# Seven block products instead of eight in a gated-MLP kernel's spatial product, with the gate branch moved ahead of it and staged in DRAM

## Chip, cores and metric

One core of one Trainium2 chip. The metric is the device time of one execution in microseconds (us). The span that a profile gives is 1.8 us shorter than the time of its run. Most runs of a kernel agree within 1%.

## The reference

```python
x = A_x                                  # (1, 2048, 576) bf16
xn = layernorm(x)
s = irfft2(rfft2(xn) * (w_r + 1j * w_i)) # a spectral filter, in six steps p0 to p5 of the kernel
z = gelu(xn @ w_in)                      # w_in: 576 x 4608
z1, z2 = z[..., :2304], layernorm(z[..., 2304:])
g = w_sp @ z2 + b_sp[:, None]            # w_sp: 2048 x 2048, the spatial product
out = x + s * silu((z1 * g) @ w_out)     # w_out: 2304 x 576
```

The spatial product is 2048 x 2048 x 2304, by far the largest of the four.

## The kernel before

z2 is computed first and stays in SBUF. The spatial product runs for four quarters of the output positions (512 columns each) and 18 feature blocks of 128. Each of these 72 steps also computes its own block of z1 one step ahead; the filter's last steps p4 and p5 fill the first steps.

```python
def z1(k):                                   # 5 matmuls of 512 columns
    ...
    nc.scalar.activation(out=Z1T[k % 3], in_=ph[:], func=ACT.Gelu_apprx_tanh)

def main(k, between=()):                     # 16 matmuls of 512 columns
    q, fi = steps[k]
    pg = psh.tile([P, 512], F32, tag="h")
    for m in range(MT):
        ...
        nc.tensor.matmul(pg[:], lhsT=Z2[m][:, fi * P:(fi + 1) * P], rhs=SLAB[q % 2][:, m, :],
                         start=(m == 0), stop=(m == MT - 1))
    nc.vector.tensor_tensor(out=tmp, in0=pg[:], in1=BB[:, q * 512:(q + 1) * 512], op=ALU.add)
    nc.vector.tensor_tensor(out=U[k % NU], in0=tmp, in1=Z1T[k % 3], op=ALU.mult)
# ... schedule, cut:
for k in range(NK):                          # 72 steps
    units = au[3 * k:3 * k + 3]              # p4 and p5 of the filter, in the first 10 steps
    ...
    if q + 1 < NQ and fi >= sl0 and fi < sl0 + 4:
        load_slab(q + 1, [fi - sl0])         # transposing loads of w_sp, into the other of two buffers
    if k + 1 < NK:
        z1(k + 1)
    main(k, units[1:])
    if fi == 0 and q > 0:
        for i in range(4):
            outm(q - 1, i)                   # 36 matmuls of 288 columns, then tanh, s and x
```

Of the kernel before, what the change touches and what calls it, by code (L numbers as in the profile page):

```python
# [79 lines left out]
def kernel(  # L80
# [25 lines left out]
    NQ = S // 512  # L106
# [18 lines left out]
    Yd = dram.tile([S, D], BF16)  # L125

# [5 lines left out]
    xnT = pers.tile([P, MT, KS, P], BF16)  # L132
    Z2 = [pers.tile([P, Fh], BF16, name=f"z2_{m}") for m in range(MT)]
    RW = pers.tile([P, KS * Fh], BF16)
# [10 lines left out]
    sizes = dict(A0=12288, G4=N2 * P, CESO=NLC * 2 * L, MM=3 * P, XN=3 * KS * P, STG=6 * L,  # L145
                 AIN=4 * 8 * L, PAD=3568, TT=8 * L, BES=2 * 8 * L, ZT=4 * 512)
# [6 lines left out]
    def reg(name, off, n):  # L153
# [7 lines left out]
    SLAB = [reg("AIN", 2 * 8 * L, 8192).rearrange("p (m t) -> p m t", m=MT),  # L161
            reg("A0", 0, 8192).rearrange("p (m t) -> p m t", m=MT)]
# [8 lines left out]
    BB = reg("TT", 0, S)  # L171
    BES = [reg("BES", i * 8 * L, 8 * L) for i in range(2)]
    WIN1 = [reg("BES", i * KS * WG * P, KS * WG * P).rearrange("p (k f) -> p k f", k=KS) for i in range(2)]
    Z1T = [reg("ZT", i * 512, 512) for i in range(3)]
    TMP = [reg("ZT", 3 * 512, 512), reg("BES", 2 * KS * WG * P, 512)]
    WOUT = reg("A0", 8192, FT * D).rearrange("p (f d) -> p f d", f=FT)
    fin = [reg("A0", 8192 + FT * D + i * D, D) for i in range(6)]
    YIN, XIN, GO = fin[0:2], fin[2:4], fin[4:6]
    WIN2 = RW[:].rearrange("p (k f) -> p k f", k=KS)
    NU = KS * Fh // 512  # L180
    U = [RW[:, i * 512:(i + 1) * 512] for i in range(NU)]

    warm = Z2[MT - 1][:, 0:512]
# [127 lines left out]
    def p4_read(ch):  # L311
        nc.sync.dma_start(out=AIN[ch % 2], in_=rowv(Ed)[:, ch * 8 * L:(ch + 1) * 8 * L])

    def p4(u):
        ch, lc = u // NLC, u % NLC
        av = AIN[ch % 2].rearrange("p (s l) -> p s l", s=8)
        pa = psa.tile([P, 2, 4, P], F32, tag="a")
        for i in range(8):
            nc.tensor.matmul(pa[:, i // 4, i % 4, :], lhsT=av[:, i, LC0[lc]:LC0[lc] + P], rhs=G4[:, ch * 8 + i, :],  # L319
                             start=True, stop=True)  # L320
        vd = V[:, lc, :, ch * 8:ch * 8 + 8, :].rearrange("p c s t -> p s c t")
        vs = pa[:].rearrange("p a s (c t) -> p (a s) c t", c=2)
        if u % 2 == 0:
            nc.vector.tensor_copy(out=vd, in_=vs)
        else:
            nc.scalar.activation(out=vd, in_=vs, func=ACT.Identity)
        if lc == NLC - 1 and ch < 2:
            p4_read(ch + 2)
# [3 lines left out]
    def p5(j):  # L332
        pa = psa.tile([P, 2, 512], F32, tag="a")
        for c in range(2):
            for lc in range(NLC):
                nc.tensor.matmul(pa[:, c, 0:L], lhsT=V[:, lc, c, 2 * j:2 * j + 2, :], rhs=CESO[:, lc, c, :],  # L336
                                 start=(lc == 0), stop=(lc == NLC - 1))
        ob = TH[:, j % 2, 0:L]
        nc.scalar.activation(out=ob, in_=pa[:, 1, 0:L], func=ACT.Identity)
        y = STG[j % 3][:, 0:D]  # L340
        nc.vector.tensor_tensor(out=y[:, 0:L], in0=pa[:, 0, 0:L], in1=ob, op=ALU.add)
        nc.vector.tensor_tensor(out=y[:, L:D], in0=pa[:, 0, H2 - 1:0:-1], in1=TH[:, j % 2, H2 - 1:0:-1], op=ALU.subtract)
        for h in range(2):
            nc.sync.dma_start(out=Yv[2 * j + h], in_=y[h * N1:(h + 1) * N1, :])

    junk = TH[:].rearrange("p a d -> p (a d)").bitcast(BF16)
# [4 lines left out]
    def z2(u):  # L351
# [10 lines left out]
        zc = Z2[m][:, n * ZC:(n + 1) * ZC]  # L362
        if on_act:
            nc.scalar.activation(out=zc, in_=ph[:], func=ACT.Gelu_apprx_tanh, accum_out=st[:, n:n + 1])  # L364
            if n % 2 == 1:
                i = NZC + n // 2
                nc.scalar.activation(out=junk[:, 0:2 * ZC], in_=Z2[m][:, (n - 1) * ZC:(n + 1) * ZC], func=ACT.Square,  # L367
                                     accum_out=st[:, i:i + 1])
        else:
            nc.scalar.activation(out=zc, in_=ph[:], func=ACT.Gelu_apprx_tanh)  # L370
            stats_q.append((u, partial(nc.vector.bn_stats, out=st[:, n, :], in_=zc)))
# [3 lines left out]
    stats_q = []  # L375

    def z2_norm(m, st, on_act):
# [9 lines left out]
        else:  # L387
            nc.vector.bn_aggr(out=mv[:, 0, :], in_=st[:])
        rs = rstd_of(mv, 1, "l2")
        stats_q.append((m * NZC + NZC + 1, partial(nc.vector.tensor_scalar, out=Z2[m][:], in0=Z2[m][:], scalar1=mv[:, 0, 0:1],  # L390
                                                   scalar2=rs[:], op0=ALU.subtract, op1=ALU.mult)))

# [6 lines left out]
    def load_slab(q, parts=range(4)):  # L399
        for i in parts:  # L400
            t0 = q * 512 + i * P
            nc.sync.dma_start_transpose(out=SLAB[q % 2][:, :, i * P:(i + 1) * P], in_=wspv[t0:t0 + P, :, :])

    steps = [(q, fi) for q in range(NQ) for fi in range(FT)]

    def z1(k):
        q, fi = steps[k]
        g = (q * FT + fi) // WG
        wb = WIN1[g % 2]
        ph = psh.tile([P, 512], F32, tag="h")  # L410
        for ks in range(KS):
            nc.tensor.matmul(ph[:].rearrange("p (a t) -> p a t", a=4), lhsT=wb[:, ks, (fi % WG) * P:(fi % WG + 1) * P],  # L412
                             rhs=xnT[:, 4 * q:4 * q + 4, ks, :], start=(ks == 0), stop=(ks == KS - 1))
        nc.scalar.activation(out=Z1T[k % 3], in_=ph[:], func=ACT.Gelu_apprx_tanh)  # L414

    def main(k, between=()):
        q, fi = steps[k]
        between = list(between)
        pg = psh.tile([P, 512], F32, tag="h")
        for m in range(MT):  # L420
            if m % 8 == 0 and between:
                between.pop(0)()
            nc.tensor.matmul(pg[:], lhsT=Z2[m][:, fi * P:(fi + 1) * P], rhs=SLAB[q % 2][:, m, :],  # L423
                             start=(m == 0), stop=(m == MT - 1))
        tmp = TMP[k % 2]
        nc.vector.tensor_tensor(out=tmp, in0=pg[:], in1=BB[:, q * 512:(q + 1) * 512], op=ALU.add)  # L426
        nc.vector.tensor_tensor(out=U[k % NU], in0=tmp, in1=Z1T[k % 3], op=ALU.mult)  # L427

    def load_xy(m):
        nc.sync.dma_start(out=YIN[m % 2], in_=Yd[m * P:(m + 1) * P, :])  # L430
        nc.sync.dma_start(out=XIN[m % 2], in_=xv[:, m, :])

    def outm(q, i):
        m = 4 * q + i
        b = m % 2
        cols = [(0, D)] if m < MT - 1 else [(0, H2), (H2, H2 + H2 // 2), (H2 + H2 // 2, D)]
        for c0, c1 in cols:
# [4 lines left out]
            for fi in range(FT):  # L442
                for h in range(nh):
                    nc.tensor.matmul(pv[:, h, :], lhsT=U[(q * FT + fi) % NU][:, i * P:(i + 1) * P],  # L444
                                     rhs=WOUT[:, fi, c0 + h * H2:c0 + h * H2 + w // nh], start=(fi == 0), stop=(fi == FT - 1))
# [5 lines left out]
            nc.sync.dma_start(out=out2[m * P:(m + 1) * P, c0:c1], in_=GO[b][:, c0:c1])  # L451
        if i < 2:
            load_xy(m + 2)
# [7 lines left out]
    NK = len(steps)  # L461
    zq = iter(range(MT * NZC))

    def fill(n, norm=True):
        for u in zq:
            z2(u)
            if norm:
                z2_stats(u)
            n -= 1
            if n == 0:  # L470
                break
# [27 lines left out]
    with tc.manual_schedule(engines={SP, PE, DVE}):  # L499
# [3 lines left out]
        load_w(1)  # L503
        fill(14)
# [9 lines left out]
        for hh in range(0, N2, 2):  # L514
# [3 lines left out]
            fill(1)  # L518
            p3(hh)
            if hh % 4 == 2 and hh >= 16:  # L520
                load_slab(0, [hh // 4 - 4])
        for i in range(2):
            nc.gpsimd.memset(WIN1[i][KT:P, KS - 1, :], 0.0)
        p4_read(0)
        p4_read(1)
        load_win1(0)
        load_win1(1)
        nc.sync.dma_start(out=BB, in_=B_b_sp.rearrange("(a s) -> a s", a=1).to_broadcast((P, S)))
        fill(MT * NZC)
        z2_stats(MT * NZC)  # L530
        z1(0)
        au = [partial(p4, u) for u in range(4 * NLC)] + [partial(p5, j) for j in range(MT)]
        LAST = (len(au) - 1) // 3
        for k in range(NK):
            q, fi = steps[k]
            units = au[3 * k:3 * k + 3]
            if units:
                units[0]()
            if k == LAST + 1:
                nc.sync.dma_start(out=WOUT, in_=B_w_out.rearrange("(f p) d -> p f d", p=P))  # L540
            sl0 = LAST + 2 if q == 0 else 2
            if q + 1 < NQ and fi >= sl0 and fi < sl0 + 4:
                load_slab(q + 1, [fi - sl0])
            if k + 1 < NK:
                z1(k + 1)
            z2_stats(MT * NZC + 9 * (k + 1))
            main(k, units[1:])
            if fi % WG == 1 and k // WG + 2 < NK // WG:
                load_win1(k // WG + 2)
            if fi == FT - 2:  # L550
                load_xy(4 * q)
                load_xy(4 * q + 1)
            if fi == 0 and q > 0:
                for i in range(4):
                    outm(q - 1, i)
        for i in range(4):
            outm(NQ - 1, i)


# [28 lines left out]
```

## Time and profile before

| | before |
|---|---|
| time, median of the first 4 runs | 552.93 us |
| span of the profiled run, granted clock | 551.1 us, 0.998 |
| TensorE busy | 540.0 us (98%), 3156 matmuls |
| VectorE busy | 221.6 us (40%) |
| spatial product | 1152 matmuls at 215.9 ns, 248.7 us |

Busy time of TensorE overstates the work, because the ends of pipelined matmuls are modelled. What counts is the distance from one matmul's start to the next (its pitch).

### The profile page before, as it was taken

The numbers are of one execution on the slowest core, as the hardware profiler recorded it, in microseconds if no ns is written. First come the engines' busy times: TensorE is split into PE (matmuls) and PEld (weight loads), VectorE is DVE, ScalarE is ACT, GpSimd is POOL, SyncE is SP. The second block draws the span as 40 slices with busy tenths as digits, with TensorE's granted clock in tenths as the row PEclk, the third lists the DMA queues.
The fourth block names the chain that finished last, engine by engine and source line by source line (L and its number), as shares of the span: only waits on it lengthen the run. The fifth ranks groups of instructions, "written<-read, shape, count | busy, mean of one in ns | idle before, by whom it ended". The sixth has DMA issues, their size and how long they took to land.

```text
span 551.1 us, 7917 instructions
## 1 busy us (share of the span) xinstructions
PE 540.0 (98%) x3156; PEld 300.2 (54%) x3156; DVE 221.6 (40%) x440; ACT 169.8 (31%) x353; POOL 41.5 (8%) x105
## 2 busy tenths in 40 slices
PE   6999999999999999999999999999999999999997
PEld 3876656665555544476444446744444574444465
DVE  5914678968545522223222222322222233222224
ACT  4788887875332211111111110111111111111101
POOL 3852111111000000000000000000000000000000
PEclk9999999999999999999999999999999999999999
DMA  9826489996304397213811120283111121112002
GB/s 307 274 88 233 166 230 267 204 205 193 119 23 101 99 272 154 75 34 91 180 33 32 33 75 2 87 179 71 32 33 44 32 76 43 33 33 77 0 1 86
DMA packets 77813, 59.50 MB, mean 108 GB/s; under 512 B 37200, under 2 KB 71888, under 8 KB 77520
## 3 DMA queue, kind: packets, MB, share of 16 engines
q1 hardware_dynamic: 76864, 56.60, 37.9%
q0 software_dynamic: 768, 2.37, 1.4%
q8 instruction: 24, 0.39, 0.3%
q14 instruction: 13, 0.11, 0.1%
q10 hardware_dynamic: 144, 0.03, 0.0%
HBM read 38.78 MB, written 11.82 MB: 92 GB/s over the span
## 4 chain that ended last, share of the span: by engine, by line
PE 88%; ACT 4%; DVE 2%; DMA 2%; issue 1%; POOL 1%; SPq 0%; DVEq 0%; POOLq 0%
PE pg L423 45%; PE ph L412 14%; PE po L444 12%; PE ph L360 8%; PE pa L251 3%; PE pa L336 2%; ACT z L364 2%; DMA AR<-in_A_w_i_dram 1%; ACT TH L367 1%; PE pa L319 1%; DMA AR<-in_A_x_dram 1%; PE pl L444 1%; PE pb L305 1%; PE pt L242 1%; ACT AR L271 1%
## 5 line engine op out<-in xcount | busy, mean ns | idle before, releaser
L423 PE MATMUL pg<-AR,z 128*128 128x512 bf16 x1152 | 261.7, 379 | 0.0
L423 PEld LDWEIGHTS <-z 128*128 128x128 bf16 x1152 | 112.3, 98 | 132.3
L426 DVE TENSOR_TENSOR AR<-pg,AR 128x512 bf16<-128x512 f32 x72 | 49.8, 692 | 212.3 <-PE pg L423 212.3
L414 ACT ACTIVATE AR<-ph 128x512 bf16<-128x512 f32 x72 | 43.0, 597 | 236.9 <-PE ph L412 236.7
L412 PE MATMUL ph<-xnT,AR 128*128 128x512 bf16 x360 | 89.5, 379 | 0.0
L360 PE MATMUL ph<-RW,xnT 128*128 128x384 bf16 x480 | 87.0, 326 | 0.0
L444 PE MATMUL po<-AR,RW 128*128 128x288 bf16 x540 | 66.8, 286 | 0.0
L444 PEld LDWEIGHTS <-RW 128*128 128x128 bf16 x594 | 56.9, 98 | 14.6
L360 PEld LDWEIGHTS <-xnT 128*128 128x128 bf16 x480 | 46.9, 98 | 26.9
L412 PEld LDWEIGHTS <-AR 128*128 128x128 bf16 x360 | 35.0, 98 | 39.8
L427 DVE TENSOR_TENSOR RW<-AR 128x512 bf16<-128x512 bf16 x72 | 30.6, 426 | 6.6
L447 ACT ACTIVATE TH<-po 128x576 f32<-128x576 f32 x15 | 9.8, 652 | 73.9 <-PE po L444 73.9
L370 ACT ACTIVATE z<-ph 128x384 bf16<-128x384 f32 x54 | 25.8, 489 | 12.3 <-PE ph L360 12.3
L448 DVE SCALAR_TENSOR_TENSOR AR<-TH,po 128x576 bf16<-128x576 f32 x15 | 11.3, 754 | 44.9 <-ACT TH L447 44.9
L395 DVE BATCH_NORM_STATS2 st<-z 128x6 f32<-128x384 bf16 x54 | 26.9, 545 | 0.9 <-ACT z L370 0.7
L295 DVE TENSOR_TENSOR AR<-pa,AR 128x578 bf16<-128x578 f32 x32 | 22.7, 748 | 5.1 <-DMA AR<-in_A_w_r_dram 2.3
L251 PE MATMUL pa<-AR,xnT 128*128 128x289 bf16 x160 | 22.7, 288 | 1.6 <-ACT xnT L243 1.6
L364 ACT ACTIVATE z<-ph 128x384 bf16<-128x384 f32 x42 | 20.3, 485 | 5.7 <-PE ph L360 5.3
L395 DVE TENSOR_SCALAR z<-z,mv,rs 128x2304 bf16<-128x2304 bf16 x16 | 14.0, 876 | 10.6 <-POOL rs L213 10.6
L251 PEld LDWEIGHTS <-xnT 128*128 128x128 bf16 x160 | 15.0, 98 | 5.7 <-ACT xnT L243 2.0
L367 ACT ACTIVATE TH<-z 128x768 bf16<-128x768 bf16 x21 | 17.7, 843 | 0.6
L213 POOL TENSOR_TENSOR rs<-ve,mhalf 128x1 f32<-128x1 f32 x30 | 16.7, 556 | 2.4
(57 smaller groups left out, 262.2 us busy)
## 6 DMA issues: line engine op xcount, KB each, us to landing
AR<-in_B_w_in_dram SPq DMA_DIRECT2D x24, 384.0 KB, 3.6
AR<-in_A_x_dram SPq DMA_DIRECT2D x20, 144.0 KB, 3.3
AR<-in_B_w_out_dram SPq DMA_DIRECT2D x1, 2592.0 KB, 9.6
Ad<-AR POOLq DMA_DIRECT2D x16, 144.5 KB, 3.5
AR<-Ad SPq DMA_DIRECT2D x4, 578.0 KB, 5.8
AR<-in_A_w_r_dram SPq DMA_DIRECT2D x16, 144.5 KB, 5.0
AR<-in_A_w_i_dram SPq DMA_DIRECT2D x16, 144.5 KB, 3.9
Bd<-AR SPq DMA_DIRECT2D x4, 578.0 KB, 2.8
```

The costliest lines, as they stand in the source:

```text
L251: nc.tensor.matmul(pa[:, c, 0:L], lhsT=xnT[:, m, ks, :], rhs=CDSD[:, ks, c, :], start=(ks == 0), stop=(ks == KS - 1))
L360: nc.tensor.matmul(ph[:], lhsT=xnT[:, m, ks, :], rhs=WIN2[:, ks, n * ZC:(n + 1) * ZC], start=(ks == 0), stop=(ks == KS - 1))
L364: nc.scalar.activation(out=zc, in_=ph[:], func=ACT.Gelu_apprx_tanh, accum_out=st[:, n:n + 1])
L367: nc.scalar.activation(out=junk[:, 0:2 * ZC], in_=Z2[m][:, (n - 1) * ZC:(n + 1) * ZC], func=ACT.Square, accum_out=st[:, i:i + 1])
L370: nc.scalar.activation(out=zc, in_=ph[:], func=ACT.Gelu_apprx_tanh)
L395: stats_q.pop(0)[1]()
L412: nc.tensor.matmul(ph[:].rearrange("p (a t) -> p a t", a=4), lhsT=wb[:, ks, (fi % WG) * P:(fi % WG + 1) * P], rhs=xnT[:, 4 * q:4 * q + 4, ...
L414: nc.scalar.activation(out=Z1T[k % 3], in_=ph[:], func=ACT.Gelu_apprx_tanh)
L423: nc.tensor.matmul(pg[:], lhsT=Z2[m][:, fi * P:(fi + 1) * P], rhs=SLAB[q % 2][:, m, :], start=(m == 0), stop=(m == MT - 1))
L426: nc.vector.tensor_tensor(out=tmp, in0=pg[:], in1=BB[:, q * 512:(q + 1) * 512], op=ALU.add)
L427: nc.vector.tensor_tensor(out=U[k % NU], in0=tmp, in1=Z1T[k % 3], op=ALU.mult)
L444: nc.tensor.matmul(pv[:, h, :], lhsT=U[(q * FT + fi) % NU][:, i * P:(i + 1) * P], rhs=WOUT[:, fi, c0 + h * H2:c0 + h * H2 + w // nh], star ...
```

## The change

The intent is to save an eighth of the spatial product. Source positions, output positions and features are each halved, so that every unit is a product of two 2 x 2 block matrices; Strassen's scheme in Winograd's form makes it from 7 products and some sums. The sums of w_sp blocks (the slabs) are made once per column tile on VectorE. Of the four sums of z2 blocks, one is made early, beside p5, and three per unit. The sums of products are made on the way out of PSUM. The seven slabs need so much SBUF that tiles are 384, 384 and 256 columns wide instead of 512, there is one slab set instead of two, and xnT (which z1 needs) gives up its place. Therefore z1 is computed whole before the product, stored to DRAM and read back per unit, and p4 and p5 are done before it too. The core of the diff:

```diff
-    def main(k, between=()):
-        ... 16 matmuls of 512 columns, add of the bias, times z1
+    def slab_sums(i):                       # S2 = L21+L22, S1 = ..., per 128 columns, 4 x 1024 elements
+        for o, a, b, op in ((5, 0, 2, ALU.subtract), (2, 2, 3, ALU.add), (4, 2, 0, ALU.subtract), (6, 1, 4, ALU.subtract)):
+            nc.vector.tensor_tensor(out=SL[:, o, :, sl], in0=SL[:, a, :, sl], in1=SL[:, b, :, sl], op=op)
+    def first(u):                           # P1, one unit ahead
+        ... 8 matmuls into a
+        nc.scalar.activation(out=p1, in_=a, func=ACT.Identity)
+        for o, h in ((p1a, 0), (p1b, 1)):
+            nc.gpsimd.tensor_tensor(out=o, in0=p1, in1=BB[...], op=ALU.add)
+    def main(u):
+        prod(b, "P6", tb[u, 0])
+        add(ux, b, p1a)
+        tsum(u + 1, 0)                      # sums of z2 blocks for the next unit, 1024 elements each
+        tsum(u + 1, 1)
+        prod(c, "P5", zblk(p, 0, 1))
+        prod(b, "P7", tb[u, 1], True)       # accumulates onto P6: must wait for the add above
+        add(p1, b, p1b)
+        out_u(1, 1, c, p1)                  # add from PSUM, then times z1
+        prod(a, "P2", zblk(p, 1, 0), True)
+        out_u(0, 0, a, B[0])
+        if u + 1 < len(units) and units[u + 1][0] == it:
+            first(u + 1)
+        prod(b, "P4", tb[u, 2], True)
+        tsum(u + 1, 2)
+        out_u(0, 1, b, p1b)
+        prod(c, "P3", zblk(p, 1, 1), True)
+        out_u(1, 0, c, ux)
 # schedule
-            z1, p4, p5 inside the 72 steps; next quarter's slabs into the second buffer
+            fill(1, kinds="21"[j % 2])      # z2 and z1 alternate beside p4 and p5
+            nc.gpsimd.dma_start(out=Z1d[fi * P:(fi + 1) * P, :], in_=zs)   # z1 to DRAM
+        for u, (it, p) in enumerate(units): # 27 units
+            if u + 1 < len(units):
+                load_z1(u + 1)
+            main(u)
+            if p == NP - 1:
+                if not last_it:
+                    load_slabs(it + 1)      # only now: the one slab set comes free
+                for n, (m, h, i) in enumerate(ms):
+                    outm(m, h, i, n % 2, last_it and n == len(ms) - 1)
+                    if not last_it and n >= len(ms) - 1 - nb and n < len(ms) - 1:
+                        slab_sums(n - len(ms) + 1 + nb)
```

## The prediction

> **What bounds the kernel now.** I read the page first: the busy line, the forty slices and the chain that ended last.
>
> ```profile
> PE 540.0 (98%) x3156; PEld 300.2 (54%) x3156; DVE 221.6 (40%) x440; ACT 169.8 (31%) x353; POOL 41.5 (8%) x105
> ...
> PE   6999999999999999999999999999999999999997
> ...
> DVE  5914678968545522223222222322222233222224
> ...
> PEclk9999999999999999999999999999999999999999
> ...
> PE pg L423 45%; PE ph L412 14%; PE po L444 12%; PE ph L360 8%; PE pa L251 3%; PE pa L336 2%; ACT z L364 2%; DMA AR<-in_A_w_i_dram 1%; ACT TH L367 1%; PE pa L319 1%; DMA AR<-in_A_x_dram 1%; PE pl L444 1%; PE pb L305 1%; PE pt L242 1%; ACT AR L271 1%
> ```
>
> TensorE is on the chain for 88% of the span at full clock, and 45% of the span is one line, L423: the spatial product (w_sp times z2). VectorE is half busy or more only in the first third; after that it is at 20 to 30%. A busy PE proves little because matmul ends are modelled, so I took the real cost of a matmul from start-to-start distances in the chain in order of time.
>
> ```profile
> 117.71 15.44 PE ph L360 x95
> ...
> 225.06 3.45 PE pg L423 x16
> 229.59 3.45 PE pg L423 x16
> 234.13 3.45 PE pg L423 x16
> 237.58 17.64 PE po L444 x144
> 256.30 3.45 PE pg L423 x16
> ```
>
> One step (16 matmuls of L423 and 5 of L412, all 512 wide) takes 234.13 - 229.59 = 4.53 us: 215.9 ns each. The 95 matmuls of 384 columns take 162.5 ns each, and the 144 of 288 take 122.5 ns. All three are N/2.4 ns plus 2.5 ns; 16 x 215.9 is 3.45 us, so nothing waits. From 117.7 us on I counted everything that was left: 19 z2 units (15.4 us), 72 z1 units (77.7), p4 and p5 (5.4 + 11.8), 1152 x 215.9 ns of L423 (248.7) and the output product (70.6) sum to 429.6 us, which ends at 547.3; the last matmul of the trace ends at 547.3. So from 118 us on there is no stall at all: a matmul taken out there is worth its full pitch. Before that there are some:
>
> ```profile
> 76.00:117.70 41.70, 39.71 (x261) 25.04 (x259) 33.96 (x60) 33.66 (x84) 6.49 (x22) 1.00 0.98 244
> ```
>
> The 261 matmuls of this stretch of the window view need 96 x 122.5 + 165 x 162.5 ns = 38.6 us of 41.7, so 3.1 us are lost, with DMA at 98% and VectorE and ScalarE at 81%.
>
> **What the Trainium skill says.** "TensorE: Matmul & The Clock Gate", section "Back-to-back issue gap", gives N/2.4 + 2.5 ns for the warm gap; the three pitches above agree, and 256 columns should then take 109.2 ns. The same section says that streams with weight loads reach about 131 ns at N=512; this trace, with a weight load before each matmul, shows 215.9, so I use the first formula. "VectorE: DVE Perf Modes", section "The perf-mode tier table", says that tensor_tensor runs at 2x on bf16 in SBUF and at 1x with any PSUM operand. The group view agrees: 512 elements take 426 ns from SBUF and 692 from PSUM. "GPSIMD Engine Reference", section "Elementwise — side-by-side cycle accounting", has 4497 ns for a 2048-element two-input add; no wide add on GpSimd is in the trace of before, so 0.85 us for 384 columns and 0.6 us for 256 are estimates from that page. "SBUF — State Buffer", section "SBUF: two separate sides", says that a VectorE instruction with two SBUF inputs and a GpSimd instruction that reads SBUF lock each other out for a whole instruction. Before, GpSimd does only one- and two-column work, so its trace does not test that.
>
> **The change, part by part.** It is the seven-product block scheme (Strassen's, in Winograd's form): features, source positions and output positions are halved, and 8 block products become 7 with sums before and after.
>
> *Main product.* Out: 1152 x 215.9 ns = 248.7 us. In: 27 units (nine feature pairs by column tiles of 384, 384 and 256), each 7 x 8 = 56 matmuls. 18 units x 56 x 162.5 ns = 163.8 us; 9 units x 56 x 109.2 ns = 55.0 us. Sum 218.8 us. Saved: **29.9 us**. The arithmetic saving alone is an eighth, 31.1 us; 1.2 us go to the fixed 2.5 ns on 360 more, shorter matmuls.
>
> *VectorE in the main stage.* Durations from the group view:
>
> ```profile
> L426 DVE TENSOR_TENSOR AR<-pg,AR 128x512 bf16<-128x512 f32 x72 | 49.8, 692 | 212.3 <-PE pg L423 212.3
> L427 DVE TENSOR_TENSOR RW<-AR 128x512 bf16<-128x512 bf16 x72 | 30.6, 426 | 6.6
> L341 DVE TENSOR_TENSOR AR<-pa,TH 128x289 bf16<-128x289 f32 x16 | 7.4, 462 | 13.7 <-ACT TH L339 13.4
> L449 DVE TENSOR_TENSOR AR<-AR 128x144 bf16<-128x144 bf16 x2 | 0.5, 232 | 0.1
> ```
>
> The two PSUM sizes give 164 + 1.031 N ns, the two SBUF sizes 156 + 0.527 N ns. A unit has 6 adds from PSUM, 4 multiplications and 3 weight sums of 8 x 128 = 1024 elements (696 ns each, 2.09 us). At N=384 that is 6 x 560 + 4 x 358 + 2090 = 6.9 us beside 9.10 us of matmuls: 75% busy, hidden. At N=256 it is 6 x 428 + 4 x 291 + 2090 = 5.8 us beside 6.12 us: 95% busy, so any lock by GpSimd shows. Walking one unit: P6 ends at 0.87 us of the unit, its add must end before P7 starts at 1.75 us; P7 ends at 2.62, and P4, which writes the same bank, starts only at 4.37. The first of these is the tight one, about 0.2 us of room. I allow 0.2 us per unit in the last column tile, **+2 us**.
>
> *ScalarE and GpSimd.* One copy of P1 and two adds per unit. P1 of the next unit is computed three products before its sum is needed (2.6 to 3.9 us); copy plus first add are about 0.5 + 0.6 to 0.5 + 0.9 us. Off the path unless the lock doubles them. The first unit of each column tile has no such lead: about 0.5 us each, **+1.5 us** in all.
>
> *Slabs.* There is one slab set instead of two buffers, so the 12 transposes for the next tile can start only as products of the last unit finish.
>
> ```profile
> 259.24 7.54 SPq L402 DMA_TRANSPOSE AR<-in_B_w_sp_dram  x3
> ...
> AR<-in_B_w_sp_dram SPq DMA_TRANSPOSE x16, 5.5
> ```
>
> Issuing takes about 2.5 us per 512 KB, so about 1.3 us per new half-size transpose; 12 are 15 to 17 us. They go in the order in which their blocks come free: P1 of the last unit runs a unit early (12 us before the end), then P5, P2, P4. I expect the tenth landing, with which the first slab sum can begin, 8 to 10 us after the last product. The six output tiles that follow are 6 x 36 x 122.5 ns = 26.5 us of matmuls, and the sums are queued only after the third of them (13 us). Three groups of 4 x 0.7 us and the output work end at about 26.5 us. Just hidden; **+0.5 us**.
>
> *Moved work.* The 72 z1 units, p4 and p5 leave the stall-free stage and are done before it, alternated with z2; their TensorE time is unchanged. z1 goes to DRAM and back (9.4 MB each way). What can be lost: in p5 a pair of steps costs TensorE 2 x 0.735 + 0.81 + 1.08 = 3.36 us and VectorE 2 x (0.462 + 0.447) + 0.545 + 0.15 + 0.76 (the early difference of z2 blocks) = 3.27 us, close to a tie: **+2 us**. The last 19 z1 units run alone, 4.3 us for each staged row block of 512 KB with two buffers; a store of 5 to 6 us overruns that a little: **+1 us**. Between p2 and p3, a z1 unit replaces a z2 unit: longer on TensorE (1.08 against 0.81 us), lighter on ScalarE and VectorE, and slab transposes leave that stretch: **-1 us** of the 3.1 lost there. The ramp and the tail stay.
>
> *Sum.* 552.9 - 29.9 + 2 + 1.5 + 0.5 + 2 + 1 - 1 = 529.0 us.
>
> **The rivals.** *VectorE becomes the bound of the main stage.* For it: 95% in the last tile, and two-input VectorE instructions that must share ports with GpSimd adds. If each GpSimd add held VectorE up fully, a unit at 256 would cost 5.8 + 1.2 = 7.0 us against 6.1 (+8 us over nine units), and one at 384 6.9 + 1.7 = 8.6 against 9.1 (still hidden): 535 us. If in addition sums with strided blocks ran at 1x (1.2 us instead of 0.7), units would take 8.6 and 10.1 us: some +22 and +18 us, and nothing would be left of the gain. Against it: the blocks' inner runs are 128 contiguous bf16, which is what the 2x mode wants. *The slab reload is exposed.* If the 12 transposes started only after the last product and landed at 20 us, the sums would end at 32 us instead of 26.5 at each of two boundaries: +8 to 10 us, 538. Against it: the reload order follows the release order. *The front part stalls.* DMA was at 98% between 76 and 118 us; z1 stores of 2 MB there could starve the filter loads, and p5 could run at VectorE's pace: +5 to 8 us, 536. *Everything hides:* 523 us.
>
> **Range and chances.** 523 is the floor by arithmetic; filter-stage stalls that shrink could take 2 more off, so the low end is 521. One rival fully at work gives 535 to 538, two give 543. The 2% line is at 541.9 us; it is passed only if two rivals meet or the weight sums are slow. Faster 0.84, same 0.14, slower 0.02.
>
> **What would show it.** Right: matmuls of the main lines at 162.5 and 109.2 ns start to start, units of 9.10 and 6.1 to 6.4 us, weight sums near 696 ns, VectorE slices at 7 to 9 tenths through the main stage, no TensorE wait above 1 us at the two tile boundaries. Wrong: TensorE waits for VectorE sums in P7 of every unit, weight sums above 1 us, GpSimd adds of 1.5 us or more, a chain that passes through slab transposes or stores of z1. The sum fails most likely in the last tile, where VectorE has the least room.

## The result, and the profile after

The changed kernel took 525.76 us (median of 10 runs, the slow one among them; the nine fast ones 523.35 to 527.8, median 525.38) against 553.08 us. The ratio of the fast runs is 0.9495 (95% interval 0.9477 to 0.9512), 5.1% less. Ratios here are the mean time of one kernel's fast runs over that of the other's of the same rounds, so not quite the ratio of the medians quoted. Executions over 1.5% slower than the fastest of the same kernel are left out of the means.

The first profile of the changed kernel fell in the slow state. The profile read below is of the same kernel, run again (a0_after), at a granted clock of 1.0 and a span of 522.2 us, 28.9 us less than before. From its page, the busy line, the slices and the chain:

```profile
PE 511.3 (98%) x3516; PEld 336.2 (64%) x3516; DVE 346.5 (66%) x687; ACT 180.4 (35%) x380; POOL 121.2 (23%) x221
...
DVE  4923756854468744637777764987777736999944
...
PE 89%; DMA 4%; DVE 3%; issue 1%; ACT 1%; POOL 0%; SPq 0%; DVEq 0%; POOLq 0%; ACTq 0%
```

TensorE is still the chain, with 360 more matmuls and 29 us less busy time. VectorE is now at 7 tenths through the two wide tiles and at 9 in the narrow one. The chain in order of time (start, length, what):

```profile
252.38 1.30 PE pm L480 x8
253.68 7.80 PE pm L498 x48
261.48 1.30 PE pm L480 x8
...
299.18 10.40 PE pm L498 x64
309.58 26.46 PE po L540 x216
336.04 1.30 PE pm L480 x8
...
417.94 17.65 PE po L540 x144
445.94 0.89 DVE AR L545
448.05 1.91 PE pm L498 x16
449.96 0.87 PE pm L480 x8
...
456.07 0.87 PE pm L480 x8
```

A wide unit takes 261.48 - 252.38 = 9.10 us, which is 56 x 162.5 ns and leaves no room for a wait; nine of them take 81.9 us. At the first tile boundary the output product (L540) and the next P1 (L480) follow each other without a gap. A narrow unit takes 456.07 - 449.96 = 6.11 us, again 56 x 109.2 ns. The only interruption of the main stage is after the second boundary: a matmul of L498 starts at 448.05 after a wait that the profile puts at 1.03 us (1.20 us by the starts of the matmuls):

```profile
448.05 1.03 PE L498 MATMUL pm<-AR 128*128 128x256 bf16 x8 [1.03 <-DVE AR L502]
```

The groups concerned (mean ns of one after the comma):

```profile
L502 DVE TENSOR_TENSOR AR<-pm,AR 128x384 bf16<-128x384 f32 x72 | 40.0, 556 | 14.0 <-PE pm L498 12.7
L507 DVE TENSOR_TENSOR AR<-AR 128x384 bf16<-128x384 bf16 x72 | 30.8, 428 | 2.5
L507 DVE TENSOR_TENSOR AR<-AR 128x256 bf16<-128x256 bf16 x36 | 14.6, 405 | 1.2
L465 DVE TENSOR_TENSOR AR<-Z 128x1024 bf16<-128x1024 bf16 x27 | 18.9, 699 | 0.0
L483 POOL TENSOR_TENSOR AR<-AR 128x384 f32<-128x384 f32 x36 | 32.2, 916 | 112.9 <-DVE AR L469 102.4 <-ACT AR L481 10.5
```

Adds from PSUM (L502) and block sums of z2 (L465) have their computed lengths, 560 and 696 ns. The multiplications by z1 (L507) do not: 428 and 405 ns where 358 and 291 were computed. Durations can't simply be added up either, because neighbours overlap in the records:

```profile
462.36 0.29 DVE L507 TENSOR_TENSOR AR<-AR 128x256 bf16<-128x256 bf16 x1
462.57 0.42 DVE L502 TENSOR_TENSOR AR<-pm,AR 128x256 bf16<-128x256 f32 x1
```

The second starts 0.21 us after the first, which lasts 0.29. The thirteen VectorE instructions of a narrow unit last 6 x 420 + 4 x 405 + 699 + 692 + 684 ns = 6.2 us together, and yet VectorE is busy for only 35.34 of 37.00 us, 5.84 us per unit.

### The profile page after: what moved, and what is told of

Same layout as the page of the kernel before. It is cut to its first block, busy times and chain, and to the rows that moved or that the text cites.

```text
span 768.1 us, 9167 instructions
## 1 busy us (share of the span) xinstructions
PE 760.3 (99%) x3516; PEld 415.2 (54%) x3516; DVE 342.5 (45%) x687; ACT 186.4 (24%) x380; POOL 119.5 (16%) x221
## 4 chain that ended last, share of the span: by engine, by line
PE 98%; DMA 1%; DVE 1%; POOL 0%; issue 0%; SPq 0%; ACT 0%; POOLq 0%
PE pm L498 37%; PE ph L370 15%; PE ph L435 15%; PE po L540 13%; PE pm L480 6%; PE pa L263 3%; PE pa L346 2%; PE pb L317 2%; PE pa L331 1%; PE pl L540 1%; PE pa L305 1%; PE pa L281 1%; PE pt L254 1%; DMA AR<-in_A_x_dram 1%; DVE st L234 0%; DVE AR L250 0%
## 5 line engine op out<-in xcount | busy, mean ns | idle before, releaser
L502 DVE TENSOR_TENSOR AR<-pm,AR 128x384 f32<-128x384 f32 (+3 forms) x162 | 83.2, 513 | 175.6 <-PE pm L498 174.6
L498 PE MATMUL pm<-AR 128*128 128x384 bf16 (+1 forms) x648 | 155.9, 403 | 0.0
L498 PE MATMUL pm<-AR,Z 128*128 128x384 bf16 (+1 forms) x648 | 155.9, 403 | 0.0
L370 PE MATMUL ph<-AR 128*128 128x384 bf16 x480 | 131.1, 432 | 0.0
L435 PE MATMUL ph<-AR 128*128 128x512 bf16 x360 | 126.9, 511 | 0.0
L498 PEld LDWEIGHTS <-AR 128*128 128x128 bf16 x648 | 78.3, 121 | 62.9
L498 PEld LDWEIGHTS <-Z 128*128 128x128 bf16 x648 | 77.7, 120 | 63.0
L540 PE MATMUL po<-AR 128*128 128x288 bf16 x540 | 99.8, 369 | 0.0
L540 PEld LDWEIGHTS <-AR 128*128 128x128 bf16 x594 | 69.9, 119 | 36.3
L370 PEld LDWEIGHTS <-AR 128*128 128x128 bf16 x480 | 57.7, 121 | 55.3 <-issue 8.6
L483 POOL TENSOR_TENSOR AR<-AR 128x384 f32<-128x384 f32 (+1 forms) x54 | 43.9, 834 | 250.8 <-ACT AR L481 250.8
L435 PEld LDWEIGHTS <-AR 128*128 128x128 bf16 x360 | 43.1, 120 | 61.5 <-issue 53.2
L480 PE MATMUL pm<-AR,Z 128*128 128x384 bf16 (+1 forms) x216 | 52.1, 404 | 0.0
L507 DVE TENSOR_TENSOR AR<-AR 128x384 bf16<-128x384 bf16 (+1 forms) x108 | 36.3, 336 | 3.7
L480 PEld LDWEIGHTS <-Z 128*128 128x128 bf16 x216 | 26.2, 121 | 21.0 <-issue 0.4
```

The costliest lines, as they stand in the source:

```text
L370: nc.tensor.matmul(ph[:], lhsT=xnT[:, m, ks, :], rhs=WIN2[:, ks, n * ZC:(n + 1) * ZC], start=(ks == 0), stop=(ks == KS - 1))
L435: nc.tensor.matmul(ph[:].rearrange("p (a t) -> p a t", a=4), lhsT=wb[:, ks, (fi % WG) * P:(fi % WG + 1) * P], rhs=xnT[:, 4 * tq:4 * tq + 4 ...
L480: nc.tensor.matmul(a, lhsT=zblk(p, 0, 0)[:, s, :], rhs=SL[:, SA["P1"], s, 0:nt], start=(s == 0), stop=(s == HM - 1))
L483: nc.gpsimd.tensor_tensor(out=o, in0=p1, in1=BB[:, h * (S // 2) + t0:h * (S // 2) + t0 + nt], op=ALU.add)
L498: nc.tensor.matmul(dst, lhsT=z[:, s, :], rhs=SL[:, SA[name], s, 0:nt], start=(s == 0 and not more), stop=(s == HM - 1), skip_group_check=more)
L502: nc.vector.tensor_tensor(out=out, in0=x, in1=y, op=ALU.add)
```

## The experiments

Medians are of fast runs beside runs of the kernel before (552.7 to 553.2 us) on the same chip. Ten runs; two of them (a0_after and a1_after_again) are the changed kernel itself.

### a0_after: the changed kernel, for a profile at full clock

> The changed kernel unaltered, to have its profile at full clock (the first one fell in the slow state, granted clock 0.657). My theory (TensorE-bound main stage, sums hidden) expects 524 to 527 us, matmuls of the seven products 162.5 ns (384 columns) and 109.2 ns (256 columns) start to start, about 219 us for the 1512 of them. The rival (VectorE bounds the units) expects TensorE waits in the nine units of the last tile, units of 7 us there instead of 6.1.

Measured: 524.77 us, ratio 0.9487 (0.9451 to 0.9522). Units take 9.10 and 6.11 us: the theory holds, and the rival (units of 7 us in the narrow tile) is out.

### e1_eight_products: the moved work alone

```diff
-        prod(b, "P6", tb[u, 0]) ... seven products and their sums
+        for h in range(2):
+            for f in range(2):
+                for sh in range(2):         # 16 matmuls per output block, 64 per unit
+                    for s in range(HM):
+                        nc.tensor.matmul(a, lhsT=zblk(p, sh, f)[:, s, :], rhs=SL[:, 2 * h + sh, s, 0:nt], ...)
+                o = U[:, 2 * p + f, h, 0:nt]   # add of the bias, times z1, as in the kernel before
-        slab_sums(...), tsum(...), the early difference of z2 blocks
```

> The moved work and the new tiles are kept, the seven-product scheme is undone: eight block products per unit (64 matmuls), no block sums at all. If the gain is the arithmetic and the move is about free, 1728 matmuls take 250.1 us instead of 218.8 and the time is 31 us above the changed kernel, about 556 us, within 1% of the kernel before. If the move of z1, p4 and p5 brings part of the gain, it is below 548 us. If the block sums cost much that TensorE has to wait for, it is nearer to the changed kernel, 540 to 550 us.

Measured: 553.81 us, ratio 1.0016 (1.0003 to 1.003). Its chain:

```profile
205.87 23.74 PE ph L431 x110
229.61 93.60 PE pm L490 x576
...
349.68 93.60 PE pm L490 x576
```

Nine wide units take 93.60 us instead of 81.9, exactly 64/56. So z1 up front with 9.4 MB to DRAM and back, smaller tiles and one slab set change the time by 0.2%, and the whole gain is the arithmetic. Neither of the two other cases that were forecast (below 548 us, 540 to 550 us) came.

### e2_nt256: all tiles narrow

```diff
-    NT = 384
+    NT = 256
```

> All column tiles 256 wide: 36 units like the nine of the last tile, in which I computed VectorE as 95% busy, and three reloads of the slabs instead of two. My theory: 2016 x 109.2 = 220.2 us of matmuls, 1.4 us more, some 0.2 us per added unit (5 us), and 1 to 3 us at the extra reload: 530 to 535 us. The rival (VectorE bound at this width, GpSimd adds holding it up): 7 us per unit instead of 6.1, 27 units more, +25 us: 550 us.

Measured: 528.52 us, ratio 0.9549 (0.952 to 0.9578), 3.8 us more than a0_after. The window view over about five narrow units (us; PE, PEld, DVE, ACT, POOL busy):

```profile
240.00:271.00 31.00, 31.00 (x286) 27.79 (x285) 29.61 (x68) 1.92 (x5) 7.60 (x10) 1.00 0.15 44
```

VectorE is busy 29.61 of 31.00 us, 95.5%, and still the units inside a tile take 6.11 to 6.12 us (one takes 6.22), as two lines of its chain show:

```profile
246.07 0.87 PE pm L480 x8
...
252.19 0.87 PE pm L480 x8
```

The 3.8 us fit the 1.4 us more of matmuls and the three waits of 1.2 us after tile boundaries, where the changed kernel has one. The 0.2 us per narrow unit that I had allowed does not exist.

### e3_sums_twice: more VectorE work

```diff
+        for rep in range(2):
             if which == 0:
                 nc.vector.tensor_tensor(out=t, in0=zblk(p, 1, 1), in1=zblk(p, 0, 1), op=ALU.subtract)
             ...
```

> Each of the three weight sums of a unit is computed twice (same result), 2.09 us more of VectorE per unit: 9.0 us against 9.10 of TensorE in the 384 tiles, 7.9 against 6.12 in the 256 tile. If VectorE is hidden as computed, the 18 wide units lose 0 to 5 us and the nine narrow ones 9 x 1.8 = 16 us: 541 to 546 us. If VectorE is already the bound in all units, 27 x 2.09 = 56 us: 580 us. If it has far more room than computed (overlapping instructions), below 535 us.

Measured: 554.83 us, ratio 1.0034 (1.002 to 1.0048). This missed all three forecasts: 30 us more, not 16 to 21. The narrow units behaved about as forecast (7.81 us), but the wide ones, which should just have fitted, take 10.08 us (from 253.33 to 263.41). Two lines of its chain, its groups and a stretch of its timeline (start, length, engine, line) show why:

```profile
253.33 1.31 PE pm L481 x8
...
263.41 1.31 PE pm L481 x8
```

```profile
L508 DVE TENSOR_TENSOR AR<-AR 128x384 bf16<-128x384 bf16 x72 | 36.9, 513 | 2.5
L470 DVE TENSOR_TENSOR AR<-Z,AR 128x1024 bf16<-128x1024 bf16 x54 | 49.1, 909 | 0.9
```

```profile
275.39 1.90 POOL L484 TENSOR_TENSOR AR<-AR 128x384 f32<-128x384 f32 x2 [8.18 <-DVE AR L503]
275.41 1.11 DVE L508 TENSOR_TENSOR AR<-AR 128x384 bf16<-128x384 bf16 x1
276.44 2.12 DVE L470 TENSOR_TENSOR AR<-Z,AR 128x1024 bf16<-128x1024 bf16 x2
```

A multiplication that starts 20 ns after a GpSimd add takes 1.11 us instead of 0.36. The 909 ns of L470 are a mean over all tiles: in the wide ones its sums take 1021 ns on average, in the narrow one 686. A wide unit thus has 4 x (513 - 358) + 2 x (1021 - 690) ns = 1.28 us more of VectorE (the next expectation, with 909, has 1.06), and VectorE is busy for 39.08 of the 40.31 us of four wide units.

### e4_sums_twice_no_gpsimd: the same without the GpSimd adds

```diff
-        nc.scalar.activation(out=p1, in_=a, func=ACT.Identity)
-        for o, h in ((p1a, 0), (p1b, 1)):
-            nc.gpsimd.tensor_tensor(out=o, in0=p1, in1=BB[...], op=ALU.add)
+        for o in (p1a, p1b):
+            nc.scalar.activation(out=o, in_=a, func=ACT.Identity)
```

> e3 with the two GpSimd adds of each unit taken out: ScalarE copies P1 twice from PSUM instead, the bias is left off, so the result is wrong on purpose. VectorE's list of instructions is that of e3. Theory (lock): in e3 two-input VectorE instructions were stretched by the GpSimd adds (513 instead of 358 ns, 909 instead of 690 ns, together 1.06 us per wide unit), which took VectorE from 9.0 to over 9.1 us; without them the wide units go from 10.08 to 9.1 us, the narrow ones from about 8.5 to 7.9 us: about 552 - 18 - 5 = 529 to 536 us. Rival (VectorE's own work alone is too long, or its order makes TensorE wait): wide units stay near 10 us, 548 us or more.

Measured: 535.13 us, ratio 0.9676 (0.9656 to 0.9695); the result is wrong.

```profile
L507 DVE TENSOR_TENSOR AR<-AR 128x384 bf16<-128x384 bf16 x72 | 25.8, 358 | 2.5
L470 DVE TENSOR_TENSOR AR<-Z,AR 128x1024 bf16<-128x1024 bf16 x54 | 37.2, 689 | 0.9
```

Both instructions are back at the lengths computed from the kernel before, the wide units at 9.10 us (242.88 to 251.98 in the chain), and 19.7 us of the 30 are gone with an unchanged list of VectorE instructions. That GpSimd instructions hold up two-input VectorE instructions is therefore shown here. What is left, 10.4 us, is the narrow tile: eight intervals of 7.54 - 6.11 = 1.43 us, less 0.8 us of the wait after the second boundary, make 10.7 us, and 10.7 us is also the difference of the two profiled spans (532.9 and 522.2). The "about 8.5 us" that the expectation gives for the narrow units of e3 was 7.81 us in its trace.

### e5_no_gpsimd: the changed kernel without the GpSimd adds

The same edit, on the changed kernel itself.

> The changed kernel with the GpSimd adds taken out in the same way (bias left off, wrong on purpose). Theory (the lock exists but is hidden except at the second tile boundary): bf16 multiplications back to 358 and 291 ns from 428 and 405, the 1.0 us wait of TensorE after that boundary gone, all else as before: 523 to 525 us, 0.5 to 1.5 us under the changed kernel. Rival (the lock costs something in every unit): 27 x 0.2 us or more, 519 us or less.

Measured: 523.09 us, ratio 0.9457 (0.9439 to 0.9476), against 0.9487 (0.9451 to 0.9522) for a0_after: the intervals overlap. Multiplications are back at 358 and 292 ns. The wait after the second boundary is 0.8 us shorter (from the start of the output product to P1 of the second unit 31.26 us instead of 32.02) but not gone, although that had been forecast: 0.4 us stay. The medians differ by 1.7 us; the trace locates only these 0.8 us. The rival (519 us or less) is out: in the units the lock (a GpSimd instruction holding up one of VectorE) is hidden.

### e6_slabs_reversed: a later reload

```diff
-        for a in (0, 2, 1, 3):
+        for a in ((0, 2, 1, 3) if it == 0 else (3, 1, 2, 0)):
```

> The reloads of the slabs at the two tile boundaries are issued in the reverse order (the block that is released last first), so that no transpose starts before the last product but one has ended: 4 us later than in the changed kernel, where they started 5.6 us before the end of the unit. Theory (reload just hidden, 2 to 3 us of room): sums 2 us later at the first boundary, less at the second with its 8 transposes: 2 to 4 us in all, 526 to 529 us. The rival of the prediction (reload exposed, 8 to 10 us at each boundary): 541 us or more. If there is more room than seen: no change, 525 us.

Measured: 529.52 us, ratio 0.9571 (0.9539 to 0.9603), 4.75 us more than a0_after. From the start of the output product to P1 of the next tile's second unit it is 38.85 us at the first boundary (32.96 in a0_after), and 32.01 (32.02) at the second. The chain and the timeline at the first:

```profile
324.64 4.58 DMA AR<-in_B_w_sp_dram
```

```profile
329.24 1.42 DVE L426 TENSOR_TENSOR AR<-AR 128x1024 bf16<-128x1024 bf16 x2 [2.69 <-DMA AR<-in_B_w_sp_dram]
```

The first slab sum waits 2.7 us for its transposes, and the output work queued behind it on VectorE waits too. The reload of 12 transposes has no 4 us of room, the one of 8 has. Both forecasts were off: more than mine, less than the rival's. Not all of the 5.9 us lost at the first boundary are waits: after a wait of 3.5 us there the next ten matmuls have twice the usual distance, at a granted clock of 0.50 (window 343.2 to 346.4), which costs 1.6 us.

### b1_first_early: an attempt at the last wait

```diff
                 for n, (m, h, i) in enumerate(ms):
+                    if not last_it and n == len(ms) - 1:
+                        first(u + 1)
                     outm(...)
```

> An attempt at a better version, right result: at a tile boundary the first product P1 of the next tile is computed before the last output tile instead of after it, so that the GpSimd adds that follow it are over when that output tile's VectorE work starts. Theory (the one wait of TensorE in the main stage is made by these adds): the 1.03 us wait after the second boundary goes, 1 us less than the changed kernel, 523.5 us. Rival (the wait comes from the slab sums ahead of it on VectorE): it stays, 524.8 us.

Measured: 527.44 us (523.65 to 530.87), ratio 0.9535 (0.9501 to 0.9568): not better, and above both forecasts (523.5 and 524.8 us). The wait after the second boundary stayed, at 0.85 us by the profile: the GpSimd adds now fell on the output tile before, and VectorE, which still had the last output tile's work ahead of the first sum, was no earlier. In the profiled run the first boundary lost 6.4 us besides, and the chain went through a load of x:

```profile
328.06 0.46 DVE L546 TENSOR_TENSOR AR<-AR 128x576 bf16<-128x576 bf16 x1 [2.35 <-DMA AR<-in_A_x_dram]
```

```profile
341.19 2.72 PE L498 MATMUL pm<-AR 128*128 128x384 bf16 x8 [3.45 <-DVE AR L426]
343.70 2.77 PE L498 MATMUL pm<-AR,Z 128*128 128x384 bf16 x8
...
347.85 1.46 PE L498 MATMUL pm<-AR,Z 128*128 128x384 bf16 x8
```

Of the 6.4 us, 3.6 are the wait itself; the rest is the clock, as in e6: up to 346.8 the matmuls start 0.32 us apart instead of 0.16, at a granted clock of 0.50. In these two runs a wait of 3.5 us on TensorE thus cost more than its own length; the wait of 1.2 us in a0_after left the clock at 1.0.

The load of x is in the changed kernel too (5.99 us to landing in a0_after); here it took 9.95 us beside the slab reload. Whether the edit made this more frequent, or this run met what any run may meet, is not settled by six runs.

### a1_after_again and b2_reload_first: the reload ahead of the z1 loads

```diff
-            if u + 1 < len(units):
+            if u + 1 < len(units) and p < NP - 1:
                 load_z1(u + 1)
 ...
                     load_slabs(it + 1)
+                    load_z1(u + 1)
```

> The changed kernel once more, with more rounds, as the neighbour of the next run: 523.5 to 528 us, with a spread of some 3 us as before, partly from the granted clock in the first 40 us and, as the reversed reload and the early P1 showed, partly from the slab reload at the first tile boundary, which has little room.

> The changed kernel with one line moved: in the last unit of a tile the loads of z1 for the next tile are issued after the slab reload instead of ahead of it, so that the reload does not wait behind them in the issuing queue. In the changed kernel the first transpose was issued 5.6 us before the end of the unit although P1, which frees its block, had ended 10 us before. Theory (the reload is near the path and its lateness makes part of the spread): the reload starts 3 to 5 us earlier, the first boundary never waits, 523 to 525 us and less spread. Rival (spread is only the clock): same times as its neighbour.

Measured: 523.94 us (523.0 to 524.97), ratio 0.9467 (0.944 to 0.9494), for the repeat, and 523.95 us (523.66 to 524.47), ratio 0.9468 (0.9445 to 0.9491), for b2: the same time. The issuing queue of a0_after first, then that of b2:

```profile
303.95 17.79 SPq L416 DMA_TRANSPOSE AR<-in_B_w_sp_dram  x12
```

```profile
299.29 17.24 SPq L416 DMA_TRANSPOSE AR<-in_B_w_sp_dram  x12
```

The reload starts 10 us before the end of the unit (309.66) instead of 5.6, and b2's first boundary has no wait, while the profiled run of the repeat lost 1.2 us there to a late store of an output tile. So the mechanism works, but in four runs of each kernel no gain in time is measured; the narrower spread is too little to call. No version that beats the changed kernel was found.

## Why the prediction was right

The range held (525.8 in 521 to 543), and the direction and the mechanism of the gain were right. The median was 3.2 us below the forecast of 529.0, because most of the charges for waits were not needed. By its own terms:

- **Main product, -29.9 us.** Right. Pitches of 162.5 and 109.2 ns, units of 9.10 and 6.11 us. e1 isolates the product: 29.0 us between the medians of e1 and a0_after, all of the gain. By the pitches it should be 31.3 us (250.1 - 218.8); 1.2 us of the difference are the wait after the second boundary, which e1 doesn't have, and the remaining 1.1 us are not located.
- **Last tile, +2 us.** Wrong: 0. The load of VectorE came out as computed (5.8 of 6.12 us, 95%; measured 95.5%), but with luck: each multiplication was on average 114 ns longer than computed, and the overlap of neighbours, which the prediction did not count, took about as much off again. The load cost nothing: the tightest sum, which has the one product between P6 and P7 (0.87 us) to be ready, ended 0.17 us before P7 started (466.22 and 466.39 in the timeline of a0_after), close to the 0.2 us of room that the prediction gave it. In e2, 31 of 36 such units run without a wait; four of the others are the first units of their tiles.
- **Tile starts, +1.5 us.** Two of three starts cost nothing; the one of the narrow tile 1.2 us, of which 0.8 go with the GpSimd adds (e5); the rest fits the output work ahead of the first sum on VectorE, but no run takes that away. With 1.03 us by the profile this wait just misses the prediction's own sign "no TensorE wait above 1 us".
- **Reload, +0.5 us.** 0 in the profile of a0_after, 1.2 us in that of the repeat. One step of the working was wrong: P1 of the last unit ended eight products or 10.4 us before the end, not 12, and the first transpose started 5.6 us before the end, because the issuing queue stood at the z1 loads (b2). Ten of the twelve transposes took the 1.3 us of the forecast to issue, the last two 2.3 and 1.9. The tenth landed 12.2 us after the last product (at 321.76), not 8 to 10, and 3.4 us before the first slab sum started (325.18). The reload is nearer to the path than I said; e6 shows how near.
- **p5, +2 us.** Wrong: 0. Pairs take 3.38 us, against 3.36 of TensorE work. The tie was not there: VectorE is busy for 21.40 of the 27.00 us of eight pairs, 79% and 2.7 us per pair where 3.27 were computed. The durations alone add up to 24.8 us; neighbours that overlap in the records explain the rest.
- **Last z1 units, +1 us, and the front, -1 us.** With every matmul of this part counted at N/2.4 + 2.5 ns, the stretch before the main stage lost 12.6 us in a0_after (227.68 - 215.05) and the stretch up to 117.71 lost 13.0 before (117.71 - 104.75). Of the 12.6, 0.4 are at a store of z1. Both terms were smaller than I gave. The chain does pass through that store (7.17 us from 206.65), which the prediction had named as a sign of being wrong; most of it was hidden.

Together -29.9 + 1.2 + 0.4 - 0.7 = -29.0, against 28.9 us between the two spans. The largest error is one habit: VectorE's load was taken as the sum of whole durations, and a place where it came near TensorE's time got a charge. The two charges of that kind, 4 us together, were both zero: in p5 VectorE was not near, and in the last tile it was near at no cost.

The rival "VectorE becomes the bound" was the right one to fear: the lock is real (e3, e4) but adds, in the changed kernel, 4 x 70 ns to a wide unit and 4 x 114 ns to a narrow one on average, not a whole GpSimd add each time, since GpSimd ran beside the adds from PSUM, which kept their 556 ns. The rival "sums with strided blocks at 1x" is out (699, 692 and 684 ns). The rival of a starved front is out (e1 and a0_after).

## What to carry to other kernels

When one engine is the bound without gaps, removing its instructions is worth their start-to-start pitch, and an engine beside it may be 95% busy at no cost as long as each result is ready in time (here the tightest had 0.17 us to spare); once it no longer fits, every microsecond counts, as e3 showed. Before adding work to VectorE, add what GpSimd will hold it up: here two-input bf16 instructions from SBUF lengthened (513 ns instead of 358 in e3), adds from PSUM did not (552 ns). A single-buffered operand that is reloaded behind the last use needs the issuing queue free at that moment, so look at what stands ahead of it in that queue, even if in b2 the earlier start brought no time.

## What the Trainium skill lacked or had wrong

- "TensorE: Matmul & The Clock Gate", section "Back-to-back issue gap", says that streams of weight load and matmul sustain about 131 ns at N=512 and 81 ns at N=128. Here, with a weight load before each matmul, the start-to-start distance is 215.9 ns at 512 and 162.5, 122.5 and 109.2 ns at 384, 288 and 256: the formula that the section calls isolated, N/2.4 + 2.5, holds in the stream.
- The same page knows clocks of 4/8 and 8/8, and 13/16 with three busy cores. A one-core run here had a mean granted clock of 0.657 for its whole 768 us (0.65 in each window after the first 76 us); no page has that state.
- "SBUF — State Buffer", section "SBUF: two separate sides": the exclusive lock agrees with the traces (1.11 us for an instruction of 0.36 us beside a GpSimd add, and 358 ns again without the adds). What it lacks is the size in a mixed stream: on average 70 to 114 ns per multiplication in a0_after, and in the wide tiles of e3 155 ns per multiplication and 331 ns per sum of L470.
- "GPSIMD Engine Reference", section "Elementwise — side-by-side cycle accounting": a two-input add is measured there at 2048 elements only. Here 384 elements took 916 ns and 256 took 775, beside VectorE's traffic, where proportion to that figure would give 843 and 562.
- "DMA: Bandwidth & Descriptors", section "Latency and other measured facts", gives 261 GB/s for a transposing load. Here 12 loads of 256 KB each, beside other transfers, were issued in 17.24 to 17.79 us, an estimate of 177 to 182 GB/s from those numbers; the median issue of 1.32 us gives an estimate of 199 GB/s.
